# Filler matmuls between two inverse stages: 34 become 27

## The chip, the cores and the metric

The kernel runs on one core of one Trainium2 chip. The metric is device time in microseconds (us) of one execution; the median of several executions is compared. The engines of a core are named as in the profile: PE (TensorE matmul), PEld (TensorE weight load), DVE (VectorE), ACT (ScalarE), POOL (GpSimd), SP (SyncE, here only a DMA queue).

## The reference

A layer norm of the rows of A_q, a gated long convolution by FFT, a residual, and then a token-mixing MLP with its own layer norms and a second residual. Cut to what matters:

```python
def _A_ref(q, k, v, shift_k, ssm_k, ssm_D):
    ...                                  # k_shift: 4-tap causal filter of k
    kv = k_shift * v
    kv_f = rfft(kv padded to 2 S);  kf_f = rfft(ssm_k padded to 2 S)
    y = irfft(kv_f * kf_f)[:S].astype(bfloat16) + kv * ssm_D
    return q * y

h  = A_q + _A_ref(_layernorm(A_q), A_k, A_v, A_shift_k, A_ssm_k, A_ssm_D)
x  = _layernorm(_layernorm(h))
u  = gelu(einsum("bsd,sf->bdf", x, B_w1) + B_b1)
h2 = h + (einsum("bdf,fs->bds", u, B_w2) + B_b2).transpose(0, 2, 1)
```

S is 2048, D is 448, F is 1792; everything is bfloat16 outside the sums.

## The kernel before

The 2048 positions are laid out as 16 rows r of 128 partitions, 448 channels wide. The FFT is done by matmuls in two stages with a shuffle of partitions between them: forward stages for the filter and for kv, a product per frequency (DVE, L1015), a first inverse stage "i1" (PE, L1027), a shuffle, and a second inverse stage "i2" (PE, L1118). The shuffle is made of DMAs from one place of the on-chip memory to another: the ordinary ones are issued by POOL and SP at L1051, the eight of the last pair at L1040 by POOL, SP and ACT. Every row of i2 reads what all shuffles have written, so none of its 32 matmuls can start before the last of them has landed.

After i2 each row r goes through a chain over four engines:

- two matmuls into one PSUM bank (L1118). Row 4 waits for the gate of row 1, row 5 for that of row 2, and from row 6 on each row waits for the gate of the row before it;
- the gate (L1125), `A = psum * scale + 1` with the scale of `qs` for that row, planned for ACT or DVE (in this profile ACT ran all 16);
- the combine (L1132) on DVE, and the statistics of the layer norm: for rows 0 and 1 on DVE (L1138, L1140), for the others a squaring on ACT (L1148) and small POOL instructions (L1155 to L1160, L1164, L1167);
- the normalised row Q (L1173, DVE), which seven matmuls of the MLP's first product use (L1218; these are 112 in all, half of that product).

`qs` holds the statistics of the rows of A_q. They are made by "q": per row one pass of DVE (L1083) with a small one after it (L1085), and per pair of rows two small POOL instructions (L1088, L1091). The other half of the first product (L1228) and the second product (L1238) follow, with DVE adding the residual (L1242) and SP writing out.

Filler matmuls compute nothing that is used: `emit_warm(n, t0, after)` issues n matmuls of 128x448 into one PSUM bank (L1061). There are three groups: N_WZ of them after the last matmul of i1, N_WI = 6 after row 3 of i2, and N_WJ = 8 after row 5 of i2.

The order of the instructions on each engine isn't written out by hand. Every instruction is recorded with `op` along with a due time `sch.t0`, and `_Sched.schedule` plays the program through with costs of its own when it is built: whenever an engine is free, it takes the ready instruction with the earliest due time (the longer remaining path breaks ties). That order, the choice of ACT or DVE, and the PSUM banks are then fixed in the program, and at run time each engine works through its instructions in order. A matmul of n columns is charged by

```python
        if W == "pe":
            if kind == "tr":
                return 70.0
            return 30.0 + n / 2.8
```

and a DMA by 600 ns of its queue (820 on POOL), and then, before its data are taken as landed, by

```python
                        d0 = free_at[e] + 1300.0
                        s = max(d0, fab)
                        fab = s + o.nbytes / (235.0 if o.keng == 8 else 410.0)
                        fin = max(fab, s + o.nbytes / (o.keng * 26.0))
                        fin += 700.0
```

The due times that matter: fillers of the first group T_I2 - 50 and up, rows of i2 T_I2 + 0.401 r with T_I2 = 85.76, pairs of "q" T_Q + 14.35 g with T_Q = 83.98.

Of the kernel before, what the change touches and what calls it, by code (L numbers as in the profile page):

```python
# [491 lines left out]
def bass_sequential_preLN__ssm_conv_h3__mixer_token_mlp__prompt_kernel(  # L492
    nc,
    A_q,
    A_k,
    A_v,
    A_shift_k,
    A_ssm_k,
    A_ssm_D,
    B_x,  # L500
    B_w1,
    B_b1,
    B_w2,
    B_b2,
    out,
):
    _build(nc, A_q, A_k, A_v, A_shift_k, A_ssm_k, A_ssm_D, B_w1, B_b1, B_w2, B_b2, out)


def _build(nc, A_q, A_k, A_v, A_shift_k, A_ssm_k, A_ssm_D, B_w1, B_b1, B_w2, B_b2, out):  # L510
# [55 lines left out]
    with ctx:  # L566
# [75 lines left out]

        T_TH, T_TN = -36.0, -30.0
        T_CP, T_XL, T_WB = 20.0, -35.53, 154.44
        N_WZ, N_WI, N_W0, N_WK, N_WJ = 34, 6, 9, 3, 8

        def evac(dst, src, w, b, n, scale=None, engs=FX, r=(), est=None):

# [649 lines left out]
```

## Time and profile before

| | us |
|---|---|
| median of 5 executions | 190.52 |
| lowest, highest | 188.67, 191.36 |
| the profiled execution, its own time | 189.64 |
| its span, first to last instruction | 187.8 |
| PE busy | 174.1 (93%) |
| DVE, ACT, POOL busy | 110.1, 97.4, 71.4 |
| mean granted TensorE clock | 1.000 |

The profiled execution took 189.64 us, of which the trace covers 187.8; the other 1.84 us lie around the span. A matmul's record in the trace is longer than its step, since matmuls are pipelined: 448 columns are recorded at some 0.352 us, while the next matmul of a stream starts 0.19 us later. So the fill of a stage is read from the starts of its matmuls and not from the busy share.

### The profile page before, as it was taken

What the parts mean: (1) busy time and instruction counts of PE and PEld (TensorE: products, weight loads), DVE (VectorE), ACT (ScalarE), POOL (GpSimd) and SP (SyncE); (2) the same over time, 40 slices, a digit from 0 to 9 for tenths busy, and PEclk for the clock granted to TensorE, in tenths of its full rate; (3) what the DMA queues carried; (4) which work ended last, traced back from release to release, by engine and by line L of the source; (5) the groups of instructions that cost most, each with busy time, mean ns of one, the idle gap of its engine ahead of it and who ended that gap; (6) DMA issues with size and microseconds to landing.
All of it is one profiled execution on the core that took longest, in us unless ns stands there. A gap on an engine that the chain in (4) does not pass through costs nothing.

```text
span 187.8 us, 2835 instructions
## 1 busy us (share of the span) xinstructions
PE 174.1 (93%) x1033; PEld 91.5 (49%) x1033; DVE 110.1 (59%) x181; ACT 97.4 (52%) x141; POOL 71.4 (38%) x177
## 2 busy tenths in 40 slices
PE   7998897988987989898989999999999999999993
PEld 2752343433332433243425444555556777777772
DVE  8877999787789999996779756000000222212221
ACT  3597989978889989940887384352121000000000
POOL 8937976779520044587168667000000000000000
PEclk9999999999999999999999999999999999999999
DMA  5997688887449916874899999900000100111111
GB/s 170 414 418 275 184 239 241 235 229 214 134 135 382 338 52 187 235 192 126 285 397 401 422 420 423 391 10 0 0 0 3 49 15 34 49 52 49 49 49 49
DMA packets 15893, 35.44 MB, mean 189 GB/s; under 512 B 3901, under 2 KB 10062, under 8 KB 15878
## 3 DMA queue, kind: packets, MB, share of 16 engines
q1 hardware_dynamic: 11222, 25.66, 36.1%
q0 software_dynamic: 4608, 9.56, 18.4%
q8 instruction: 8, 0.13, 0.3%
q14 instruction: 7, 0.06, 0.1%
q10 hardware_dynamic: 48, 0.03, 0.0%
HBM read 22.37 MB, written 1.84 MB: 129 GB/s over the span
## 4 chain that ended last, share of the span: by engine, by line
PE 74%; ACT 8%; DMA 8%; DVE 7%; issue 2%; SPq 0%; ACTq 0%
PE ps L1238 23%; PE ps L1228 11%; PE ps L1218 10%; DMA arena<-arena 8%; PE ps L1027 5%; PE ps L885 5%; ACT arena L652 4%; PE ps L964 4%; PE ps L1118 3%; PE ps L933 3%; PE ps L904 3%; PE ps L914 3%; ACT arena L943 3%; DVE arena L1015 2%; PE ps L1061 2%
## 5 line engine op out<-in xcount | busy, mean ns | idle before, releaser
L1242 DVE SCALAR_TENSOR_TENSOR arena<-ps,arena 128x448 bf16<-128x448 f32 x16 | 10.9, 684 | 56.9 <-PE ps L1238 56.9
L1238 PE MATMUL ps<-arena 128*128 128x448 bf16 x224 | 42.5, 352 | 0.0
L1238 PEld LDWEIGHTS ps<-arena 128*128 128x128 bf16 x224 | 32.3, 144 | 10.1
L943 ACT CAST arena<-ps 128x896 bf16<-128x896 f32 x32 | 26.8, 926 | 3.8 <-PE ps L933 1.7
L652 ACT CAST arena<-ps 128x896 bf16<-128x896 f32 (+1 forms) x26 | 22.0, 908 | 2.5 <-PE ps L868 1.6
L1218 PE MATMUL ps<-arena 128*128 128x448 bf16 x112 | 23.0, 353 | 0.3 <-DVE arena L1173 0.2
L947 POOL DMA_DIRECT2D arena<-arena x32 | 19.3, 603 | 8.2 <-ACT arena L943 5.5
L1228 PE MATMUL ps<-arena 128*128 128x448 bf16 x112 | 21.4, 352 | 0.0
L964 PE MATMUL ps<-arena 128*64 128x448 bf16 x128 | 16.4, 362 | 2.4 <-ACT arena L652 1.0
L1208 ACT ACTIVATE arena<-ps,arena 128x448 bf16<-128x448 f32 x14 | 8.2, 640 | 20.1 <-PE ps L1228 14.7
L879 DVE TENSOR_TENSOR arena<-arena 128x1792 bf16<-128x1792 bf16 x16 | 18.2, 1176 | 0.2 <-DMA arena<-in_A_k_dram 0.2
L1125 ACT ACTIVATE arena<-ps,arena 128x448 f32<-128x448 f32 x16 | 11.2, 722 | 13.0 <-PE ps L1118 10.0
L933 PE MATMUL ps<-arena 128*128 128x448 bf16 x64 | 16.0, 355 | 1.3 <-ACT arena L943 1.3
L1015 DVE TENSOR_TENSOR arena<-arena 128x1792 bf16<-128x1792 bf16 x16 | 16.4, 1083 | 0.0
L885 PE MATMUL ps<-arena 128*128 128x448 bf16 x64 | 14.6, 354 | 1.9 <-ACT arena L943 1.3
L1218 PEld LDWEIGHTS ps<-arena 128*128 128x128 bf16 x112 | 10.9, 98 | 11.1 <-DVE arena L1173 1.3
L1051 POOL DMA_DIRECT2D arena<-arena x14 | 8.2, 590 | 20.8 <-PE ps L964 15.6
L1228 PEld LDWEIGHTS ps<-arena 128*128 128x128 bf16 x112 | 11.0, 98 | 10.2
L1027 PE MATMUL ps<-arena 64*128 64x448 bf16 x128 | 14.1, 351 | 1.3 <-DVE arena L1015 0.6
L1132 DVE SCALAR_TENSOR_TENSOR arena<-arena 128x448 f32<-128x448 bf16 x16 | 10.7, 677 | 5.5 <-ACT arena L1125 5.5
L964 PEld LDWEIGHTS ps<-arena 128*64 128x64 f16 x128 | 5.4, 108 | 12.1 <-ACT arena L652 4.6
L655 DVE CAST arena<-ps 128x896 bf16<-128x896 f32 (+2 forms) x11 | 9.5, 875 | 2.7 <-PE ps L868 1.2
(88 smaller groups left out, 199.7 us busy)
## 6 DMA issues: line engine op xcount, KB each, us to landing
arena<-arena POOLq DMA_DIRECT2D x46, 196.0 KB, 5.5
arena<-in_B_w_dram SPq DMA_DIRECT2D x8, 896.0 KB, 9.3
arena<-in_B_w_dram SPq DMA_DIRECT2D x2, 2048.0 KB, 17.1
arena<-in_B_w_dram SPq DMA_DIRECT2D x2, 1536.0 KB, 19.9
arena<-in_A_k_dram SPq DMA_DIRECT2D x4, 448.0 KB, 7.2
arena<-in_A_v_dram SPq DMA_DIRECT2D x4, 448.0 KB, 7.8
arena<-in_A_q_dram SPq DMA_DIRECT2D x4, 448.0 KB, 4.7
out_dram<-arena SPq DMA_DIRECT2D x7, 224.0 KB, 1.9
```

The lines of the kernel that those rows point to most:

```text
L652: return e.copy(out=dst(), in_=src())
L879: op("dve", lambda e, W, T=T, i=i, r=r: e.tensor_tensor(out=T[:, i], in0=KH[:, r:r + 4, :], in1=WT, op=ALU.mult), r=[(o_KH + r * DB, 4 * D ...
L885: op("pe", lambda e, W, b=b, T=T, i=i, j=j: e.matmul(Pb(b, i), ID, T[:, i, j, :], start=(j == 0), stop=(j == 3)), r=[(o_ID, 256), (o + (i ...
L933: op("pe", lambda e, W, b=b, r=r, h=h, dl=dl: e.matmul(Pb(b, h), E[:, 2 * r + h, :], src[:, r, :], start=True, stop=not dl), r=[r_E(r), (o ...
L943: return e.copy(out=dst, in_=Ppair(b)) if W == "act" else e.tensor_copy(out=dst, in_=Ppair(b))
L947: shuf[tag + q_ + str(r)] = shuf[tag + q_] = op(q_, lambda e, W, w=w, p0=p0, a=a, b_=b_, j0=j0: e.dma_start(T[p0:p0 + 29:4, j0:j0 + (b_ - ...
L964: op("pe", lambda e, W, b=bs[h], h=h, j=j, c=c, par=par: e.matmul(PS[64 * par:64 * par + 64, b.slots[c], 0:D], FW[:, 64 * c:64 * c + 64], ...
L1015: op("dve", lambda e, W, m=m, i=i: e.tensor_tensor(out=MR(m.slots[0]).rearrange("p (x y) d -> p x y d", x=2), in0=TU[:, i].unsqueeze(2).br ...
L1027: k = op("pe", lambda e, W, b=bs[h], m=ms[h], par=par, t=t, tab=tab, xy=xy, P=P: e.matmul(Pb(b, par), tab[P, :], MR(m.slots[0])[P, xy, :], ...
L1218: op("pe", lambda e, W, r=r, fc=fc, b=bs[fc]: e.matmul(Pb(b), W1A[:, r, 128 * fc:128 * fc + 128], Q[:, r, :], start=(r == 0), stop=(r == R ...
L1228: op("pe", lambda e, W, r=r, fc=fc, b=b: e.matmul(Pb(b), W1B[:, r, 128 * (fc - n0):128 * (fc - n0) + 128], Q[:, r, :], start=(r == 0), sto ...
L1238: op("pe", lambda e, W, r=r, fc=fc, b=b: e.matmul(Pb(b), W2[fc // 7][:, fc % 7, r:S:R], G[:, fc, :], start=(fc == 0), stop=(fc == NFC - 1) ...
```

## The change

One constant: the first filler group, between i1 and i2, has 27 matmuls instead of 34. The other two groups and everything else in the text of the kernel stay. Since the order is made by `_Sched.schedule` from all instructions, it is made anew for the changed list.

```diff
         T_TH, T_TN = -36.0, -30.0
         T_CP, T_XL, T_WB = 20.0, -35.53, 154.44
-        N_WZ, N_WI, N_W0, N_WK, N_WJ = 34, 6, 9, 3, 8
+        N_WZ, N_WI, N_W0, N_WK, N_WJ = 27, 6, 9, 3, 8
```

The group is emitted by this line of the list PLAN, ahead of i2:

```python
                ("warm", emit_warm, (N_WZ, T_I2 - 50.0, lambda: i1_last[-1:])),
```

## The prediction

> **What bounds the kernel now.** I read the slices of the page first, then the chain of waits around the change, then the timeline there, then the waits of PE.
>
> ```profile
> PE   7998897988987989898989999999999999999993
> PEclk9999999999999999999999999999999999999999
> DMA  5997688887449916874899999900000100111111
> ```
>
> PE is nearly full in every slice and the last third is PE alone. But seven or eight tenths in the middle are partly fillers. The chain says what the end hangs on:
>
> ```profile
> 82.42 0.67 SPq L1040
> 83.09 0.04 issue
> 83.14 5.60 DMA arena<-arena
> 88.74 0.09 issue
> 88.83 1.69 PE ps L1118 x8
> 90.52 0.05 issue
> 90.56 1.31 PE ps L1061 x6
> 91.87 0.77 PE ps L1118 x4
> ```
>
> Columns are start, length, what. Between i1 and i2 the path is one shuffle: issued by SP at 83.09, landed 5.60 us later. The first filler group isn't on it; the other two groups (L1061 x6, and x8 later) are. The timeline shows the group itself (start, length, engine, what, in brackets the idle time before it):
>
> ```profile
> 81.36 6.61 PE L1061 MATMUL ps<-arena 128*128 128x448 f16 x34
> 86.49 1.12 DVE L1083 BATCH_NORM_STATS2 arena<-arena 128x6 f32<-128x448 bf16 x2
> 88.83 1.48 PE L1118 MATMUL ps<-arena 128*128 128x448 bf16 x7 [0.86 <-DMA arena<-arena]
> 90.17 0.69 DVE L1132 SCALAR_TENSOR_TENSOR arena<-arena 128x448 f32<-128x448 bf16 x1 [2.56 <-ACT arena L1125]
> 92.91 0.56 ACT L1148 ACTIVATE arena<-arena 128x448 bf16<-128x448 f32 x1
> 93.47 0.71 ACT L1125 ACTIVATE arena<-ps,arena 128x448 f32<-128x448 f32 x1
> ```
>
> The fillers end at 81.36 + 6.61 = 87.97 and PE then idles 0.86 us for the DMA. So already before the change the last filler ends ahead of the landing. DVE has finished its statistics at 87.6 and idles 2.56 us for the first gate.
>
> From 88.83 to the last L1238 at 184.96, 96.13 us, PE issues 32 L1118, 14 fillers, 112 L1218, 112 L1228 and 224 L1238: 494 matmuls. At the step of the filler group, (6.61 - 0.352) / 33 = 0.190 us, they need 93.7 us. So PE has 2.4 us of idle time behind the landing, all of it before 113.27; from there it runs through. From the starts in the timeline I place it: 0.2 ahead of each small filler group, 0.85 around 94.4 to 95.6, 0.8 around 97.4 to 98.35, 0.4 at 112.9. The waits name the cause, the gates:
>
> ```profile
> PEld ps L1118 <- ACT arena L1125: 3.3, 8, 0.9
> ```
>
> **What the Trainium skill says.** TensorE: Matmul & The Clock Gate, Back-to-back issue gap, prices a warm matmul at N/2.4 + 2.5 ns, for 448 columns 189 ns; the trace's 0.190 agrees. The same page, Part 1: The HAM clock gate, says that PE falls to half its clock after an idle window of about 3.4 us and needs about as long of work to come back. The trace shows that state only at the start: the first nine L904 take 3.54 us, 0.39 each, the page's N/1.2 = 0.373 and a little. The granted clock in the page reads 9 there too, so that row doesn't show this state; the step of the matmuls does. The page also says, in Architectural detail: the array is 16x 32x32, that ACT and DVE are strictly first in, first out, which is why an instruction planned one place later matters.
>
> **The change part by part.** *Seven fillers removed.* 7 x 0.190 = 1.33 us less PE work, ending at 86.64 instead of 87.97. All of it lies beside the shuffle, so it is worth nothing: the landing at 88.74 depends on SP's issue and on the DMA, and neither waits for a filler. PE's idle time before i2 becomes 0.86 + 1.33 = 2.19 us. The cover for the zero is the shuffle; a gain would need a landing before 87.97, over 0.77 us earlier than here, and then could at most be that excess. No DMA, PSUM bank release or wait of another engine hangs on the fillers.
>
> *The longer idle time.* It isn't shown before: PE's longest idle stretch, apart from the start, is 1.03 us. Bounds: nothing, if 2.19 us are too short for the gate (the page's 3.4 us, taken plainly); or half clock for some 3.4 to 5 us, which spans 9 to 13 matmuls, each 0.20 dearer, 1.8 to 2.6 us, less some 0.3 to 0.5 where PE would have idled for a gate. I take nothing and keep +2.3 for the range.
>
> *The order made anew.* This is the only thing that can move the end otherwise. By the planner's own costs (these are its plan, not times of the chip) the 34 fillers fill 34 x 0.19 = 6.46 us, while the last shuffle is taken as landed earlier: three POOL issues of 0.82 begin some 0.4 after the fillers, so 0.37 + 3 x 0.82 + 1.3 + about 0.7 for the data and its queue + 0.7 = 5.5 us. So in the old plan i2 waited for the fillers, for 0.95 us. With 27 fillers they end at 5.13, and i2 starts with the landing, 0.95 planned us earlier against the statistics "q", which don't move. Playing the queue on from there by hand, I get three moves:
> - DVE: 12 passes L1083 stood before the first combine L1132; now 11, and the twelfth follows it. On the chip that pass (0.608 mean, a step of 0.57 to 0.6) leaves an idle stretch of 2.56 us and enters one in which DVE is busy without a gap from 90.17 to 96.4; a small L1085 (0.12) leaves it in turn. So the first Q comes 0.45 us later, and the seven L1218 behind it.
> - ACT: the gate of row 5 goes ahead of the first squaring L1148. In the trace that squaring (92.91) stands before the gate (93.47). Row 5's gate comes up to 0.5 us earlier, the squares 0.7 later.
> - PE: row 6 is ready sooner, and goes ahead of the last filler of the third group: one step, 0.19 earlier. Row 7 may come ahead of the first L1218, which then wait behind it.
>
> What waits: L1218 for Q (+0.45), rows for gates (-0.2), PE behind row 7 (0 to +0.2). Since PE is full from 98.7 to 112.5 and again from 113.27, idle time that is added or saved in the first ten us stays to the end. Sum: +0.45 - 0.2 + 0.1 = about +0.3; but part of the late Q is covered by fillers and by the gate waits, so I take +0.2. Ends: every further row that slips behind a gate costs the step of the chain, 1.37 us (94.24, 95.61, 96.98, 98.35 are the starts of rows 6 to 9); at best the order closes all 2.4 us of idle time. So -2.4 to +2.7 (two slips), mostly -0.6 to +1.2.
>
> Against the profiled execution: 189.64 + 0.2 = 189.84. It lies 0.88 under the median of the runs, so 190.52 + 0.2 = **190.7**.
>
> **The rivals.**
> 1. *Nothing moves at all* : fillers off the path and an order that is equal where it counts: 190.5. For it: the 0.86 us of idle. Against: the plan's i2 start does move by 0.95.
> 2. *PE goes cold in the gap* : slower. From the point where 2.19 us of idle time (or the few matmuls around it) count as an idle window, the 26 matmuls from 88.83 on begin at 0.39 instead of 0.19. +1.3 to +2.6, 191.8 to 193.1, at the middle 192.5. For it: 36% of the 3.4 us ahead of the landing are then filled, (86.64 - 85.4) / 3.4, and nothing before it is so thin. Against: the price in the skill is a whole window.
> 3. *The order falls badly* : a gate or a POOL step of "q" gets behind something late, and one or two rows slip: +1.4 to +2.7, 191.9 to 193.2. For it: ACT once waited 2.6 us for L1091 in the trace, just covered by 30 L1218.
> 4. *The order falls well* : gates go ahead of squares all along, rows come sooner and the two stretches of 0.8 close: -1 to -2.4, 188.1 to 189.5. For it: rows 6 to 9 are paced by gates alone. Against: the same squares feed the Q that PE needs.
>
> That the change doesn't do what it says is part of all of these: the last filler will end 2.1 us before the landing rather than with it.
>
> **How the numbers follow.** My forecast with rival 1: 0.58 (its own range 189.9 to 191.7). Cold PE 0.16, bad order 0.12, good order 0.14. One per cent, about what a measurement of this kernel can tell from no change, is 188.6 and 192.4. Slower by more: half of the cold case, half of the bad order and 0.08 of what the runs' own spread of 1.4% adds: 0.23. Faster by more: half of the good order and 0.06 of the spread: 0.13. Within: 0.64. For 8 in 10 the range leaves out the outer part of the good order and of the two slow cases: 188.7 to 192.9.
>
> **What would show it.** 27 L1061 in the first group, ending near 86.6 against a landing at 88.7, with an idle time of about 2.2 us ahead of L1118. If the first L1118 step by 0.19, PE stayed warm; 0.39 would prove rival 2. One L1083 directly behind the first L1132 and the first L1218 near 95.1 would prove the DVE move; a gate ahead of the first L1148 the ACT move. The last two products, L1228 and L1238, should keep their 21.2 and 42.4 us. I am wrong if the landing itself moves by more than 0.5 us, or if PE's idle time between the landing and the start of L1228 differs from 2.4 us by more than 1.2.

## The result, and the profile after

The changed kernel takes 190.93 us in the median of 44 executions, the kernel before 189.94 in that of 79. The ratio is **1.0085, with an interval from 1.0068 to 1.0103**: slower by 0.85%, about 1.6 us. The ratio is that of the means of the fast executions, those at most 1.5% above the fastest of their kernel (34 of the 44 and 44 of the 79), which is why it isn't the quotient of the two medians, 0.99 us apart. The profiled execution of the changed kernel has a span of 190.1 us against 187.8.

The slices, for all of the span; they tell little:

```profile
PE   7998897698988989896969998999999999999993
PEclk9999999999999999999999999999999999999999
```

A slice is 4.75 us long. PE is emptier in slices 19 and 21, which read 6 where both read 8 before: the idle time ahead of the landing lies in 19, the first rows behind it in 21. The granted clock is still 9 everywhere. The chain of waits of the changed kernel (start, length, what) says more:

```profile
83.67 1.25 SPq L1040
84.92 0.04 issue
84.96 4.35 DMA arena<-arena
89.31 0.09 issue
89.40 1.69 PE ps L1118 x8
91.09 0.04 issue
91.13 1.31 PE ps L1061 x6
...
95.17 0.73 ACT arena L1125
95.91 0.04 issue
95.95 0.57 PE ps L1118 x2
96.52 0.02 issue
96.54 0.73 ACT arena L1125
...
114.71 0.73 ACT arena L1125
115.45 0.04 issue
115.49 0.55 PE ps L1228 x2
116.05 7.94 PE ps L1218 x42
123.99 20.81 PE ps L1228 x110
144.80 42.39 PE ps L1238 x224
```

Between i1 and i2 it is the shuffle as before. Behind the landing the chain passes through four gates on ACT, at 95.17, 96.54, 99.28 and 114.71 (before through three, at 94.83, 97.57 and 111.33), and two L1228 now stand ahead of 42 L1218. I call the time from the start of the first L1118 to the end of the last L1238 **the stage**. After the change it is 144.80 + 42.39 - 89.40 = **97.79 us**; before it was 96.13. So 1.66 of the 2.3 us between the spans lie behind the landing, and that is also the size of the ratio's 1.6. The rest lies ahead of it: the first filler starts 1.25 us later (82.61 against 81.36), in a part in which neither an instruction nor the planned order of any engine was changed, and i2 follows 0.68 us sooner on it (6.79 against 7.47). Over all runs shown below that issue fillers, i2 started 6.3 to 7.8 us after the first one, for 34 fillers as for 27, so that part is spread and not the change. The stage, by contrast, came out the same to 0.01 us in both pairs of runs below that ran one order with different numbers of fillers, 27 and 34, so the experiments are read by it.

The timeline of the changed kernel, with the lines that answer to those of before:

```profile
82.61 5.28 PE L1061 MATMUL ps<-arena 128*128 128x448 f16 x27
89.40 1.67 PE L1118 MATMUL ps<-arena 128*128 128x448 bf16 x8 [1.51 <-DMA arena<-arena]
90.74 0.69 DVE L1132 SCALAR_TENSOR_TENSOR arena<-arena 128x448 f32<-128x448 bf16 x1 [2.40 <-ACT arena L1125]
91.34 0.62 DVE L1083 BATCH_NORM_STATS2 arena<-arena 128x6 f32<-128x448 bf16 x1
92.86 1.34 ACT L1125 ACTIVATE arena<-ps,arena 128x448 f32<-128x448 f32 x2 [0.31 <-PE ps L1118]
94.09 0.57 ACT L1148 ACTIVATE arena<-arena 128x448 bf16<-128x448 f32 x1
111.94 2.24 PE L1218 MATMUL ps<-arena 128*128 128x448 bf16 x11
113.36 0.70 ACT L1125 ACTIVATE arena<-ps,arena 128x448 f32<-128x448 f32 x1
115.49 0.55 PE L1228 MATMUL ps<-arena 128*128 128x448 bf16 x2 [0.82 <-ACT arena L1125]
```

The first three moves of the order that were forecast are there: one L1083 behind the first combine; two gates (rows 4 and 5) ahead of the first squaring; and row 6 ahead of the last small filler. The last three lines are a fourth, further down the order: the gate of row 14 (113.36) has fallen behind three squarings, row 15 behind eleven L1218, and two L1228 stand ahead of the L1218 that Q would soon allow. PE's waits show the sum of it, over the whole row chain (total, times, longest); after the change:

```profile
PEld ps L1118 <- ACT arena L1125: 5.0, 9, 1.1
PE ps L1118 <- ACT arena L1125: 1.9, 3, 0.6
PE ps L1228 <- ACT arena L1125: 0.8, 1, 0.8
```

Before, the weight loads (PEld) waited 3.3 us in eight waits, as the prediction shows, and the matmuls themselves

```profile
PE ps L1118 <- ACT arena L1125: 0.9, 2, 0.4
```

Counting matmuls at 0.19 us places the loss. Rows 7, 8 and 10 each find PE idle for their gate after the change, and row 11 starts at 107.45; before, it started at 106.31:

```profile
95.95 0.55 PE L1118 MATMUL ps<-arena 128*128 128x448 bf16 x2 [0.63 <-ACT arena L1125]
97.32 0.55 PE L1118 MATMUL ps<-arena 128*128 128x448 bf16 x2 [0.63 <-ACT arena L1125]
100.06 0.55 PE L1118 MATMUL ps<-arena 128*128 128x448 bf16 x2 [0.63 <-ACT arena L1125]
107.45 0.54 PE L1118 MATMUL ps<-arena 128*128 128x448 bf16 x2
```

```profile
106.31 0.54 PE L1118 MATMUL ps<-arena 128*128 128x448 bf16 x2
```

When row 11 starts, PE of before has issued 82 matmuls in 17.48 us from the first L1118, 1.90 of them idle; after, 80 in 18.05, 2.85 idle: **0.95** more. Between there and the last 42 L1218, the gap grows from 0.95 to 1.66: **0.71** more at the end.

### The profile page after: what moved, and what is told of

It is laid out like the page before. It is cut to its first block, busy times and chain, and to the rows that moved or that the text cites. A ratio compares the mean times of both kernels' runs of the same rounds, so it can differ in the third digit from the quotient of the medians.

```text
span 190.1 us, 2821 instructions
## 1 busy us (share of the span) xinstructions
PE 172.8 (91%) x1026; PEld 91.0 (48%) x1026; DVE 109.9 (58%) x181; ACT 97.7 (51%) x141; POOL 71.5 (38%) x177
## 4 chain that ended last, share of the span: by engine, by line
PE 67%; DMA 12%; ACT 8%; DVE 6%; POOL 3%; issue 2%; SPq 1%; ACTq 0%
PE ps L1238 22%; PE ps L1228 11%; PE ps L1218 11%; DMA arena<-arena 9%; PE ps L1027 5%; ACT arena L652 4%; PE ps L1118 4%; PE ps L964 3%; DMA arena<-in_A_ssm_k_dram 3%; POOL arena L947 2%; PE ps L885 2%; DVE arena L1015 2%; PE ps L914 2%; ACT arena L943 2%; PE ps L933 2%
## 5 line engine op out<-in xcount | busy, mean ns | idle before, releaser
L1238 PE MATMUL ps<-arena 128*128 128x448 bf16 x224 | 42.5, 352 | 0.0
L1238 PEld LDWEIGHTS ps<-arena 128*128 128x128 bf16 x224 | 32.3, 144 | 10.1
L1218 PE MATMUL ps<-arena 128*128 128x448 bf16 x112 | 22.7, 352 | 0.0
L1228 PE MATMUL ps<-arena 128*128 128x448 bf16 x112 | 21.5, 353 | 0.8 <-ACT arena L1125 0.8
L885 PE MATMUL ps<-arena 128*128 128x448 bf16 x64 | 14.5, 354 | 3.6 <-ACT arena L943 3.0
L933 PE MATMUL ps<-arena 128*128 128x448 bf16 x64 | 16.0, 355 | 1.3 <-ACT arena L943 1.3
L1228 PEld LDWEIGHTS ps<-arena 128*128 128x128 bf16 x112 | 10.9, 98 | 11.3 <-ACT arena L1125 1.3
L1218 PEld LDWEIGHTS ps<-arena 128*128 128x128 bf16 x112 | 11.0, 98 | 10.2
L888 DVE TENSOR_TENSOR arena<-ps,arena 128x896 bf16<-128x896 f32 x8 | 8.7, 1091 | 4.3 <-PE ps L885 4.2
L1118 PE MATMUL ps<-arena 128*128 128x448 bf16 x32 | 8.1, 355 | 3.4 <-ACT arena L1125 1.9
```

The source lines that it names most:

```text
L885: op("pe", lambda e, W, b=b, T=T, i=i, j=j: e.matmul(Pb(b, i), ID, T[:, i, j, :], start=(j == 0), stop=(j == 3)), r=[(o_ID, 256), (o + (i ...
L933: op("pe", lambda e, W, b=b, r=r, h=h, dl=dl: e.matmul(Pb(b, h), E[:, 2 * r + h, :], src[:, r, :], start=True, stop=not dl), r=[r_E(r), (o ...
L1218: op("pe", lambda e, W, r=r, fc=fc, b=bs[fc]: e.matmul(Pb(b), W1A[:, r, 128 * fc:128 * fc + 128], Q[:, r, :], start=(r == 0), stop=(r == R ...
L1228: op("pe", lambda e, W, r=r, fc=fc, b=b: e.matmul(Pb(b), W1B[:, r, 128 * (fc - n0):128 * (fc - n0) + 128], Q[:, r, :], start=(r == 0), sto ...
L1238: op("pe", lambda e, W, r=r, fc=fc, b=b: e.matmul(Pb(b), W2[fc // 7][:, fc % 7, r:S:R], G[:, fc, :], start=(fc == 0), stop=(fc == NFC - 1) ...
```

## The experiments

Two theories at first. *Order theory*: only the new order of the instructions costs time. *Gap theory*: PE's longer idle time ahead of i2 costs it. Two edits tell them apart: the order is planned for one number of fillers, and another number is issued. In this one the planner sees 34 fillers, and those from the 28th on are left out when the program is written:

```diff
-        order = self.schedule()
+        order, self.warm0 = self.schedule(), min([i for i in range(len(self.ops)) if self.ops[i].tag == "warm"])
-                o.ev = self.issue(W, o.fn(self.eng[W], W))
+                o.ev = _Ev(0, W, self.cnt[W]) if o.tag == "warm" and oid >= self.warm0 + 27 else self.issue(W, o.fn(self.eng[W], W))
```

**Order for 34, 27 issued.**

> The kernel before with its planned order (made for 34 fillers), but only 27 fillers of the first group issued. Order theory: only the order cost time, so this is as fast as before, ratio 1.000 within 0.4%, with 96.1 us from the first L1118 to the end of L1238 and an idle time of PE ahead of L1118 of 1.5 to 2.2 us. Gap theory (the longer idle time of PE costs): as slow as the changed kernel, ratio 1.008, and a step of L1118 above 0.19 us.

Measured: ratio 0.9988, interval 0.9959 to 1.0017. Its timeline and the end of its chain:

```profile
82.68 5.28 PE L1061 MATMUL ps<-arena 128*128 128x448 f16 x27
89.69 1.67 PE L1118 MATMUL ps<-arena 128*128 128x448 bf16 x8 [1.73 <-DMA arena<-arena]
```

```profile
143.43 42.39 PE ps L1238 x224
```

PE idles 1.73 us, and the stage is 143.43 + 42.39 - 89.69 = 96.13 us, that of before. Seven fillers less cost nothing and bring nothing here. The gap theory falls for a gap of this length.

**Order for 27, 34 issued.** The changed kernel, where the last filler is issued eight times:

```diff
-                o.ev = self.issue(W, o.fn(self.eng[W], W))
+                o.ev = [self.issue(W, o.fn(self.eng[W], W)) for _ in range(8 if o.tag == "warm" and self.ops[oid + 1].tag != "warm" else 1)][-1]
```

> The changed kernel's order (made for 27 fillers), with seven more fillers issued behind the 27th. Order theory: as slow as the changed kernel, ratio 1.008, 97.8 us from the first L1118 to the end of L1238. Gap theory: back at the time of before, ratio 1.000, 96.1 us.

Measured: stage 97.79, that of the changed kernel, with an idle time of 0.85 us. The ratio, 1.0176 (1.0119 to 1.0233), is even above that of the changed kernel; it rests on six executions, and what is above 1.0085 isn't in the stage. The profiled execution shows where such time can lie: its granted clock is at half in slices 4 and 5, far ahead of the fillers, where sixteen L933 in a row (from 17.30 on) take 6.43 us, some 0.4 each.

```profile
PEclk9985599999999999999999999999999999999999
```

The order theory holds: the whole 1.66 us belong to the order.

**Order for 34, none issued.** The first edit with 0 in place of 27.

> The order of before, with none of the first group issued: PE idles the whole shuffle, some 7 us. Here the gap theory's price must show if there is one: matmuls behind the landing at 0.39 instead of 0.19 us, 1.5 to 3 us longer from the first L1118 on, ratio 1.008 to 1.016. If fillers do nothing even here: ratio 1.000.

Measured: ratio 1.0141 (1.0087 to 1.0194), stage 98.96, 2.83 us more. Its timeline, and its slices of the granted clock:

```profile
88.12 3.15 PE L1118 MATMUL ps<-arena 128*128 128x448 bf16 x8 [7.50 <-DMA arena<-arena]
91.32 2.42 PE L1061 MATMUL ps<-arena 128*128 128x448 f16 x6
93.54 1.21 PE L1118 MATMUL ps<-arena 128*128 128x448 bf16 x4
```

```profile
PEclk9999999999999999985599999999999999999999
```

After 7.50 us of idle time eight L1118 take 3.15 us instead of 1.67, most of them 0.37 us apart instead of 0.19, and the slices 19 and 20 show half the clock. So the fillers have a use, but not down to the last seven of them.

**Which engine's order?** Two theories again. *PE theory*: PE's own order, with rows that wait for gates ahead of L1218. *Chain theory*: ACT squares row 3 later; POOL's L1160 waits for that square and stands ahead of row 1's L1167; so the second Q comes late (9.26 us behind the landing instead of 8.17), and with it all of DVE. For these runs a helper moves one instruction behind another on its own engine and leaves the rest; the pairs are the instruction and the one that it is put behind:

```diff
-        order = self.schedule()
+        order = _moved(self, self.schedule(), [(1016, 970)])
```

That is the gate of row 7 behind the squaring of row 3, in the changed kernel; the other three are changes of before: `[(977, 1023)]` the opposite exchange, `[(972, 998)]` the squaring of row 2 behind the gate of row 5, and `[(615, 953), (614, 1041)]` the forecast's DVE move. The last two ran only once, and so did the four mixed orders and the two single places further down; of these runs only the stage of the one execution is used.

> The changed kernel with one exchange in ACT's order: the gate of row 7 behind the squaring of row 3 instead of ahead of it. Chain theory (late square of row 3 holds POOL's L1160, which stands ahead of row 1's L1167, which holds the second Q and with it all of DVE): the second Q comes 0.9 to 1.2 us earlier after the landing, and the stage from the first L1118 to the end of L1238 falls from 97.79 to 96.6 to 97.0. PE theory (rows that stand ahead of L1218 in PE's order cost it): at most 0.2 us, 97.6 to 97.8.

> The kernel before with the opposite exchange: the squaring of row 3 behind the gate of row 7. Chain theory: the second Q comes about 0.7 to 1.2 us later, the stage grows from 96.13 to 96.8 to 97.3, ratio 1.003 to 1.006. PE theory: 96.1 to 96.3, since PE's order is that of before.

> The kernel before with the gate of row 5 ahead of the squaring of row 2, the ACT move of the prediction alone. Prediction: the stage from the first L1118 to the end of L1238 changes by -0.2 us (row 5's gate earlier), to 95.9. Chain theory: it is the squares that count, 96.1 to 96.5.

> The kernel before with the DVE move of the prediction alone: the twelfth L1083 behind the first L1132, and the L1085 that stood there put to the next one. Prediction: the first Q comes 0.45 us later and the stage from the first L1118 to the end of L1238 becomes 96.4 to 96.6. Chain theory: under 0.2 us, 96.1 to 96.3, since POOL and ACT and not DVE set the second Q.

Measured stages: 97.79, 96.92, 96.08 and 96.13; the ratios of the first two are 1.0069 (1.0035 to 1.0103) and 1.0090 (1.0047 to 1.0134). The second ratio is above the 0.4% that 0.79 us in the stage make up; the rest isn't in the stage of the profiled execution. In the first, Q of row 1 does come 0.84 us earlier, at 8.42, and nothing comes of it: row 11 still starts 18.05 us behind the landing, since 37 L1218 stand ahead of it on PE. In the second the late square costs 0.79 us in the order of before, and the profile shows the chain link by link:

```profile
96.34 0.20 POOL L1160 TENSOR_TENSOR arena<-arena 128x2 f32<-128x2 f32 x1 [2.40 <-ACT arena L1148]
96.49 0.57 POOL L1167 TENSOR_TENSOR arena<-arena 128x1 f32<-128x1 f32 x1
97.10 0.51 DVE L1173 TENSOR_SCALAR arena<-arena 128x448 bf16<-128x448 f32 x1 [1.93 <-POOL arena L1167]
97.67 0.36 PE L1218 MATMUL ps<-arena 128*128 128x448 bf16 x1 [1.35 <-DVE arena L1173]
```

So the chain is real, but the changed order doesn't hang on it alone: the first run came out as the PE theory had it, the second as the chain theory. The other two are the forecast's own terms: the DVE move, priced at +0.45, costs 0.00, and the ACT move, a part of -0.2, is worth 0.05.

**The orders exchanged, engine by engine.** Here `_moved` is given whole orders of engines from the other kernel's plan (`OTHER`, lists of instructions, left out):

```diff
-        order = self.schedule()
+        order = _moved(self, self.schedule(), OTHER)
```

> PE works in the order of before, ACT, DVE and POOL in that of the changed kernel. PE theory (PE's own order costs the 1.66 us): the stage from the first L1118 to the end of L1238 is 96.1 to 96.4. Chain theory (the order of ACT, DVE and POOL makes Q late): 97.0 to 97.8, with idle time of PE ahead of L1218 that ends on L1173.

> PE works in the order of the changed kernel, ACT, DVE and POOL in that of before. PE theory: 97.6 to 97.9 us for the stage. Chain theory: 96.1 to 96.4. Both together, each enough by itself: 97 or more here and in the run with the orders the other way round.

> Only ACT works in the order of the changed kernel, the others in that of before. If the squares and gates are the source of the late Q: 96.9 us (as with the square of row 3 alone) to 97.8. If DVE or POOL is: 96.1 to 96.9.

> Only ACT works in the order of before, the others in that of the changed kernel. If ACT's order is the source and nothing else: 96.1 to 96.6 us for the stage. If PE's order is enough by itself: 97.3 to 97.8.

Measured stages: 98.66, 98.40, 99.06 and 98.40. The two theories taken singly miss; "each enough by itself", with 97 or more in both exchanges, is met, but it doesn't say why every mix is slower than either kernel, by up to 2.9 us over before. In the first, PE of before finds the late Q of the others and waits 1.35 us for it, at the same L1218 as above:

```profile
98.57 0.36 PE L1218 MATMUL ps<-arena 128*128 128x448 bf16 x1 [1.35 <-DVE arena L1173]
```

In the second PE waits for gates instead (2.4 us in three waits by its list of waits). My reading is that the orders of four engines in one plan fit each other: in these mixes no engine's order was good or bad by itself, and the 1.66 us can't be shared out among the engines.

**The two places.** So I shared it out by time, and changed the order of the changed kernel at each place on the engines together. At the end: the gate of row 14 is put behind the squaring of row 11 and so ahead of those of rows 12 and 13, row 15 behind five L1218, the two L1228 behind the last L1218. In front: rows 7, 8, 9 and 10 behind two, four, none and eight L1218, and the gate of row 7 behind the squaring of row 3.

```
end:   [(1079, 1052), (1082, 1161), (1083, 1082), (1217, 1209), (1218, 1217)]
front: [(1016, 970), (1014, 1099), (1015, 1014), (1026, 1103), (1027, 1026), (1043, 1111), (1044, 1043)]
```

> The changed kernel with its last part in an order like that of before: gate of row 14 behind the squaring of row 11 and ahead of those of rows 12 and 13, row 15 behind five of the eleven L1218, the two early L1228 behind the last L1218. Two-places theory: PE's idle time of 0.98 us behind row 15 goes, stage 97.79 becomes 96.8 to 97.1. If Q of row 10 comes no sooner: 97.5 to 97.8.

> The changed kernel with its first part in an order like that of before: rows 7 to 10 behind two, four, none and eight L1218, and the squaring of row 3 ahead of the gate of row 7. Two-places theory: 0.8 us less idle time before row 11, but row 11 waits for the gate of row 10, so 0.4 us of it reach the end: 97.3 to 97.5. If the end of the stage hides it: 97.7 to 97.8.

> Both edits together. Two-places theory: 96.2 to 96.7 us for the stage, ratio 1.000 to 1.004. If the cost lies elsewhere in the order: 97.3 or more, ratio 1.007 or more.

Measured stages: 97.13, 97.40 and 96.74, that is -0.66, -0.39 and -1.05: the two add up. With both the ratio is 1.0013 (0.9970 to 1.0056). The first and the third lie 0.03 and 0.04 us outside the ranges of the two-places theory (96.8 to 97.1, 96.2 to 96.7), and far from the other ones. The end gives back nearly all of its 0.71: with the gate of row 14 earlier, Q of row 10 comes at 24.86 us behind the landing instead of 25.31, and the 42 L1218 start with it:

```profile
113.10 8.12 PE L1218 MATMUL ps<-arena 128*128 128x448 bf16 x42 [0.17 <-DVE arena L1173]
```

The front gives back 0.39 of 0.95, since row 11 then waits for the gate of row 10, as the expectation said. That gate waits in turn for POOL's L1091, a step of "q". With the front undone it starts 16.88 us behind the first L1118 (107.46 - 90.58); in the kernel before the same wait ended at 15.89 (104.72 - 88.83) and was covered by 30 L1218:

```profile
107.46 0.72 ACT L1125 ACTIVATE arena<-ps,arena 128x448 f32<-128x448 f32 x1 [2.79 <-POOL arena L1091]
108.23 0.55 PE L1118 MATMUL ps<-arena 128*128 128x448 bf16 x2 [0.24 <-ACT arena L1125]
```

```profile
104.72 0.73 ACT L1125 ACTIVATE arena<-ps,arena 128x448 f32<-128x448 f32 x1 [2.59 <-POOL arena L1091]
```

So row 11 starts at 17.65 with 80 matmuls ahead of it, against 17.48 with 82: 0.55 of the last 0.61 us against before. The trace shows this wait; an order in which L1091 comes sooner was not run.

**Orders planned for more fillers.** If the trouble is a plan in which i2 starts too early, a later start in the plan should do no harm. In the first run the order is planned for 41 fillers and 34 are issued; in the second for 36, with 34 issued and the two small groups set to 0:

```diff
-        N_WZ, N_WI, N_W0, N_WK, N_WJ = 34, 6, 9, 3, 8
+        N_WZ, N_WI, N_W0, N_WK, N_WJ = 36, 0, 9, 3, 0
```

> 34 fillers issued, in an order that was planned for 41, so that the plan starts i2 later against the statistics of A_q, as the chip does. Order theory: the plan now fits the chip better, 95.2 to 96.0 us from the first L1118 to the end of L1238, ratio 0.995 to 1.000, and not slower. Theory that any new order is worse than the one of before: ratio over 1.004.

> 34 fillers in an order planned for 36, and none of the two small filler groups inside i2 (14 matmuls, 2.7 us of PE work that the chain of waits shows on the path). If those fillers are on the path: 93.5 to 94.5 us for the stage, ratio 0.988 to 0.993. If they only stand where PE waits for gates anyway: 95.5 to 96.1, ratio 0.996 to 1.000. If PE needs them to stay at full clock: a step above 0.19 us and a ratio over 1.004.

Measured: the first has a stage of 95.96 and a ratio of 0.9990 (0.9955 to 1.0025), no difference that can be told. The second has a stage of 96.80 and a ratio of 1.0073 (1.0045 to 1.0101), again more than the 0.67 us in the stage make up: the third of its expectations. Its timeline:

```profile
92.69 0.55 PE L1118 MATMUL ps<-arena 128*128 128x448 bf16 x2 [1.91 <-ACT arena L1125]
94.06 0.55 PE L1118 MATMUL ps<-arena 128*128 128x448 bf16 x2 [0.82 <-ACT arena L1125]
94.45 1.80 PE L1218 MATMUL ps<-arena 128*128 128x448 bf16 x5
```

Five L1218 take 1.80 us instead of 1.11: behind two idle times of 1.91 and 0.82 us with only two matmuls between them PE has fallen to half its clock, and its page reads 6 for the granted clock of that slice, the 21st. So in these orders the small groups earn their place, though PE would otherwise only wait there; as the order was planned anew too, how much of the 0.67 us is the clock's isn't separated. No version tried is faster than the kernel before by more than can be told.

## Why the prediction was right or wrong

- *Seven fillers removed, worth nothing*: right. The fillers end ahead of the landing in both kernels, and the run with the old order and 27 fillers has the old stage to 0.01 us. Only with the end undone did i2 start so early, 6.29 us after the first filler, that 34 of them (6.46 us) would have held it, by some 0.2 us.
- *The longer idle time, nothing taken, +2.3 kept*: right for this gap. 1.51 us in the changed kernel (2.19 were forecast) and 1.73 with the old order left the step at 0.19. The price that was kept for the other case, 1.8 to 2.6, was a little low: without fillers it was 2.83.
- *i2 starts 0.95 planned us earlier, and the order changes*: right, and the three moves named are in the trace. Played through for both kernels, `_Sched.schedule` puts the start of i2 at 84.57 and 83.62 us of its own time.
- *"Sum: +0.45 - 0.2 + 0.1 = about +0.3", taken as +0.2*: **this is the step that failed**, and not by one term. The +0.45 of DVE is 0.00: the first Q does come 0.40 us later (5.51 against 5.11 behind the first L1118), but the two L1218 that it feeds stand in front of row 7, which waits for its gate until 6.78 in any case. The -0.2 measured -0.05 for its ACT part. The "0 to +0.2" for PE behind row 7 was the place of the loss: in the changed kernel not one row but four, 7 to 10, come ahead of L1218 that stood ahead of them before, and the 0.95 us more of idle time ahead of row 11 are PE's waits at these rows. And the playing of the queue stopped at row 7: the move of the gate of row 14 behind three squarings, with 0.71 us, stands some 20 us further down and was not looked for.
- *Idle time in the first ten us stays to the end*: half right. Undoing the front gave 0.39 of 0.95; the rest met the gate of row 10, which waited for L1091.
- *Rival 3, the order falls badly*: this is what happened, with 1.66 us inside its +1.4 to +2.7, and of its mechanism the gate that gets behind something late. "One or two rows slip" is not what it looks like: rows 7 to 10 stand further ahead in PE's order than before, and PE waited at three of them. Its reason, ACT's wait for L1091 that 30 L1218 just covered, did not cost the changed kernel anything itself, where 37 L1218 cover it; it is what keeps the front from being won back. It had a chance of 0.12. Rivals 1 and 4 fall with the longer stage, rival 2 with the step of 0.19 behind the gap.
- *The measured ratio of 1.0085 lies within the one per cent that was called most likely*, but it is clear of no change, on the side of slower, and eight times the 0.2 us that was forecast. That the median of 190.93 lies so near the forecast of 190.7 is luck: its base, 190.52 from five executions, was 0.58 above the 189.94 of 79.
- *The signs*: the first L1218, put near 95.1, started at 96.34, behind row 7. Both signs of being wrong came up. The landing moved by 0.57 us (88.74 to 89.31), which is the spread ahead of it; PE's idle time behind the landing grew from 2.40 to 4.06 us, by 1.66 where 1.2 was the limit, and that is the loss.
- *Readings and sums*: the idle stretch put at 0.85 us around 94.4 to 95.6 is 0.60 (95.61 - 94.63 less two matmuls of 0.19), and the three parts of "slower by more" add up to 0.22 and not 0.23. Neither bears on the outcome.

Why the planner makes an order that is worse: in its own account the new plan is not worse. It starts i2 0.95 us earlier, and yet the last L1238 ends at 180.92 us of its time instead of 180.91: its stage has grown from 96.35 to 97.30, since what it waits for there, the statistics of A_q, did not move. On the chip the start didn't come earlier, because i2 starts 6.3 to 7.8 us behind the first filler and not after the 5.5 at which the new plan has the shuffle landed; only the longer stage was left, and it is longer by 1.66 us and not by the plan's 0.95. That the plan's error about the landing is the cause of the whole is argued, not shown: the order planned for 41 fillers, with a later start, was no slower than before, but also not faster.

## What to carry to other kernels

Where a planner writes the order, a constant that looks like pure padding is an input to the plan: ask how long the plan believes the padding and the transfer beside it to be, and which of the two it waits for. To try such an edit, change what is issued and keep the order, then change the order and keep what is issued. And follow a re-made order to its end before pricing it: early moves can vanish in waits that exist anyway, and the one that counts can stand twenty microseconds further down.

## What the runs showed of the hardware

PE's fall to half clock is not only a matter of one long gap. A single idle time of 2.50 us behind a dense stream of 27 fillers (in the run with the front undone) left the next matmuls at 0.19 us each, while 1.91 and 0.82 us with two matmuls between them brought the step to 0.37. These are single profiled executions; the mean granted clock of the second run is 0.991 or less in 21 of its 22 executions, against 3 of 35 of the kernel before beside it. And the granted clock of the slices does show this state: 5 after the gap of 7.50 us, although the same row reads 9 at the start of the kernel before, where nine matmuls took 0.39 each; the prediction had taken that row to be blind to it.
